# Dummy transposes only in the first part of the order, and later expected landings for the loads of tiles 9 and on

## The chip, the cores and the metric

The kernel runs on one core of a Trainium2 chip. The metric is the device time of one execution in microseconds (us), the median of several runs. TensorE is called PE here, its weight loads PEld, VectorE DVE, ScalarE ACT, GpSimd POOL and SyncE SP. A "q" behind a name (SPq) is the sequencer of that engine, which issues DMAs and serves semaphores.

## The reference

A linear attention with a decaying state runs over 768 steps of 4 batches and 8 heads; its output, 3072 tokens of 384 values, goes through a feed-forward layer with silu, and then through a routed layer, in which every token visits one of 8 experts:

```python
for t in range(S):
    cur = np.einsum('bhd,bhe->bhde', u[None] * kt, vt)
    y[:, :, t] = np.einsum('bhd,bhde->bhe', rt, state + cur)
    state = w[None, :, :, None] * state + np.einsum('bhd,bhe->bhde', kt, vt)
...
h = x @ w_in
x = (h * (1.0 / (1.0 + np.exp(-h)))) @ w_out
...
logits = x @ w_gate + modality_bias[modality_id]
e_idx = np.argmax(logits, axis=1)
gate_w = probs[np.arange(N), e_idx]
for e in range(E):
    h = np.maximum(x[mask] @ w1[e], 0.0)
    out[mask] = gate_w[mask, None] * (h @ w2[e])
```

x has 3072 rows; d_model is 384, the first hidden width 2048, that of an expert 1024.

## The kernel before, in words

**Tiles.** The tokens are cut into 24 tiles of 128, and three tiles form a group j (0 to 7). For each tile, the attention part turns a load A (L284: v and the transposed r and k, 768 KB, into one of the buffers AB_132, AB_133 and "stall") and a load B (L287: r and k in natural order, 192 KB for tiles below NZ = 9, 384 KB from there) into rows of x. The steps that matter here: L460 (DVE) and L464 (POOL) scale the two halves of A; L435 and L436 (POOL) multiply r, k and u, from load B; L439 (DVE) sums them; L480 and L548 (POOL) are two more elementwise steps; L487 (PE) forms the scores and L493 (DVE) writes them under the causal mask; L503 and L544 (PE) form the output and the state.

**The first layer.** For a group and each of 16 slices of the hidden width, L618 (PE) forms the hidden values in bank ph, in nine products, as each operand is split into a high and a low part; L622 and L623 (ACT) apply silu, L625 (DVE) makes the low part gl, and L637 (PE) adds nine products into the three accumulators pa_79 to pa_81. Groups 0 and 1 are computed in two halves of the slices; after the second half L653 (DVE) adds the accumulators to the first half's result in x2all.

**Routing.** L686 (PE) transposes x2all, L697 and L702 (PE) form the logits, L714 to L720 (DVE) choose the expert, L734 (POOL) counts, L739 and L740 (PE) turn counts into ranks. L764 (SP) stores the rows of x to the buffer x_rows in DRAM, three per group; L780 (POOL) scatters the token numbers to the lists of their experts.

**The expert stage.** Nine slots of 384 tokens, each of one expert: rows of x are gathered (POOL), L949 and L957 (PE) form the two products, L961 (ACT) or L963 (DVE) scales the result by the gate, and L966 (POOL) scatters 128 rows to the output by an indirect DMA. After them L1078 opens a loop over slots that did not fit into the nine; with these inputs it is not entered, but every engine meets at it.

**What sets the order.** The class Plan is a small scheduler which runs when the program is built. Every piece of work is added with an engine, a planned duration, a priority (lower goes first), its dependencies and the buffers that it takes and frees. `order` steps a clock, and each idle engine takes the ready piece of lowest priority. A piece with nbytes is a DMA: its planned landing follows a common stream of 260 KB per us plus a constant, and its consumers become ready only then. The planned start times are then the order in which the instructions are written (L1074), and each engine executes its own instructions in that order; nothing reorders them on the chip. A piece whose planned landing is earlier than the real one therefore stands in its engine's queue and blocks what is behind it.

**Dummy transposes.** L371 to L373 add 100 blocks of four 128 x 128 transposes of the identity with priorities from 900 on, so that the planned PE takes one wherever it has nothing else that is ready:

```python
for i in range(100):
    add("PE", 0.45, 900 + i, lambda i=i: [pe.transpose(bank(("w", i))[:, 0:128], ident, ident) for _ in range(4)],
        acq=[("ha"[i % 2], ("w", i))], rel=[("w", i)], lat=0.0)
```

Their results are never read. In the plan of the kernel before, 45 blocks start between 1.0 and 118.2 us and 55 between 742 and 771 us, all of them at the end of the expert stage.

Of the kernel before, what the change touches and what calls it, by code (L numbers as in the profile page):

```python
# [16 lines left out]
SP = mybir.EngineType.SP  # L17
# [25 lines left out]
NZ = 9  # L43
# [13 lines left out]
class Plan:  # L57
# [7 lines left out]
    def add(self, eng, dur, prio, fn, deps=(), acq=(), rel=(), lat=0.2, nbytes=0):  # L65
        o = Op()
        o.eng, o.dur, o.prio, o.fn, o.lat, o.nbytes = eng, dur, prio, fn, lat, nbytes
        o.deps = [d for d in deps if d is not None]
        o.acq, o.rel = list(acq), list(rel)
        o.n, o.after, o.left = len(self.ops), [], 0  # L70
        self.ops.append(o)
        return o

    def order(self):
# [6 lines left out]
        events, dma, t, done = [], 0.0, 0.0, []  # L81
# [4 lines left out]
        while True:  # L86
            moved = True
            while moved:
                moved = False
                for e in ENGINES:  # L90
                    if busy[e] > t + 1e-9 or not ready[e]:
                        continue
                    held, pick = [], None
                    while ready[e]:
                        x = heapq.heappop(ready[e])
                        need = {}
                        for p, _ in x[2].acq:
                            need[p] = need.get(p, 0) + 1
                        if all(len(self.free[p]) >= k for p, k in need.items()):
                            pick = x[2]  # L100
                            break
                        held.append(x)
                    for x in held:
                        heapq.heappush(ready[e], x)
                    if pick is None:
                        continue
                    o = pick
                    for p, key in o.acq:
                        self.slot[key] = (p, self.free[p].pop(0))
                    o.start = t  # L110
                    busy[e] = t + o.dur
                    end = t + o.dur + o.lat
                    if o.nbytes:
                        dma = max(dma, t + o.dur) + o.nbytes / 260e3
                        end = dma + 4.0
                    heapq.heappush(events, (busy[e], count, None))
                    heapq.heappush(events, (end, count + 1, o))
                    count += 2
                    done.append(o)
                    moved = True  # L120
# [19 lines left out]
def moe_rwkv_kernel(tc, ins, out):  # L140
# [142 lines left out]
    def load_A(n, s):  # L283
        sp.dma_start(AB[s][:, 0:AW], ins["av"][n])  # L284

    def load_B(n, s, w_=0):
        sp.dma_start(AB[s][:, AW + w_ * DM:], ins["rk"][n * C:(n + 1) * C, w_ * DM:])  # L287
# [52 lines left out]
    for i in range(NP):  # L340
        n = 1 << i
# [17 lines left out]
    def sl_(key):  # L359
        return P.slot[key][1]  # L360
# [47 lines left out]
    def attention(n):  # L408
# [5 lines left out]
        if n < 3:  # L414
            P.slot[kA] = ("tA", n)
            if n < 2:
                P.free["tA"].remove(n)
            oA, oB = gate((0.1, 0.2, 2.2)[n]), add("SP", 0.5, -49 + n, lambda: load_B(n, n, 1), nbytes=200e3)
        else:
            oA = add("SP", 0.6, z - 9, lambda: load_A(n, sl_(kA)), acq=[("tA", kA)], nbytes=786e3)  # L420
            oB = add("SP", 0.6, z - 8.9, lambda: load_B(n, sl_(kA), int(n < NZ)), [oA], nbytes=393e3 if n >= NZ else 197e3)
        relA = [kA] if n != 2 else []

        def f_V():
# [648 lines left out]
        expert(s)  # L1073
    with tc.manual_schedule():  # L1074
        for o in P.order():
            o.fn()
    tn = nc.values_load(tailn, min_val=0, max_val=NMAX - NSTAT + NA + 1)
    with tc.For_i(0, tn, 1) as i:  # L1078
        e_ids("t", lists[1], bass.ds(i + (NSTAT - 1 - NA), 1))
# [91 lines left out]
```

## Time and profile before

| | us |
|---|---|
| median of 3 runs | 808.32 (807.42 to 811.14) |
| the profiled execution | 806.15 |
| its span in the profile | 804.4 |
| PE busy with products | 791.2 (98%) |
| DVE, ACT, POOL busy | 425.7, 337.3, 227.9 |
| dummy transposes L372, on the chain that ended last | 5% of the span (3% into pa, 2% into ph) |

The profile is one execution. Its page gives the busy time of each engine, the span in 40 slices of 20.1 us with the clock that was granted to TensorE, and the groups of instructions. Behind it stand views of the trace: the waits of an engine by what ended them, the timeline of a stretch, and the sums of a stretch. The clock is written as a share of full speed. Rows of the views follow below, in the order in which the prediction comes to them.

### The profile page before, as it was taken

What the parts mean: (1) busy time and instruction counts of PE and PEld (TensorE: products, weight loads), DVE (VectorE), ACT (ScalarE), POOL (GpSimd) and SP (SyncE); (2) the same over time, 40 slices, a digit from 0 to 9 for tenths busy, and PEclk for the clock granted to TensorE, in tenths of its full rate; (3) what the DMA queues carried; (4) which work ended last, traced back from release to release, by engine and by line L of the source; (5) the groups of instructions that cost most, each with busy time, mean ns of one, the idle gap of its engine ahead of it and who ended that gap; (6) DMA issues with size and microseconds to landing.
All of it is one profiled execution on the core that took longest, in us unless ns stands there. A gap on an engine that the chain in (4) does not pass through costs nothing.

```text
span 804.4 us, 15749 instructions
## 1 busy us (share of the span) xinstructions
PE 791.2 (98%) x6348; PEld 760.0 (94%) x6348; DVE 425.7 (53%) x793; ACT 337.3 (42%) x726; POOL 227.9 (28%) x280
## 2 busy tenths in 40 slices
PE   8999999998999999999999999999999999999998
PEld 7998999987999999999999999999999999999998
DVE  7989965635534543644643522353866544654310
ACT  3566765443334334334334422364435434444200
POOL 5435302343423422522421203210432313220120
PEclk9999999998999999999999999999999999999999
DMA  6454433081511411411421024531675345500000
GB/s 245 153 177 184 167 119 108 28 79 44 90 59 59 91 60 60 89 60 61 85 65 59 11 22 180 224 120 68 217 217 187 128 135 199 196 28 1 30 35 2
DMA packets 23920, 83.27 MB, mean 104 GB/s; under 512 B 7659, under 2 KB 12152, under 8 KB 21538
## 3 DMA queue, kind: packets, MB, share of 16 engines
q1 hardware_dynamic: 19730, 72.55, 30.1%
q0 software_dynamic: 3968, 9.66, 3.6%
q8 instruction: 51, 0.84, 0.5%
q14 instruction: 27, 0.22, 0.2%
q10 hardware_dynamic: 144, 0.00, 0.0%
HBM read 78.92 MB, written 9.77 MB: 110 GB/s over the span
## 4 chain that ended last, share of the span: by engine, by line
PE 90%; DVE 4%; DMA 3%; issue 1%; ACT 1%; POOL 1%; DVEq 0%; POOLq 0%; SPq 0%; ACTq 0%
PE ph L618 24%; PE pa L637 23%; PE ph L949 13%; PE pa L957 12%; PE pt L503 4%; PE pa L372 3%; PE pt L487 3%; PE ph L372 2%; DMA xgb<-x_rows,it 2%; DMA AB<-in_av_dram 1%; PE pt L933 1%; PE ph L305 1%; PE pt L686 1%; PE pt L544 1%; PE pt L697 1%
## 5 line engine op out<-in xcount | busy, mean ns | idle before, releaser
L625 DVE TENSOR_TENSOR gl<-sg,gh 128x384 fp32r<-128x384 f32 x128 | 86.7, 677 | 136.4 <-ACT gh L623 135.9
L622 ACT ACTIVATE sg<-ph 128x384 f32<-128x384 f32 x128 | 63.0, 492 | 214.0 <-PE ph L618 205.6
L637 PE MATMUL pa<-Wh,gh 128*128 128x384 f32 x384 | 132.7, 346 | 0.0
L637 PE MATMUL pa<-Wh,gl 128*128 128x384 f32 x384 | 129.7, 338 | 0.5 <-DVE gl L625 0.4
L637 PE MATMUL pa<-Wl,gh 128*128 128x384 f32 x384 | 128.8, 335 | 0.0
L618 PE MATMUL ph<-xh,Wh 128*128 128x384 f32 x384 | 92.8, 349 | 0.0
L618 PE MATMUL ph<-xh,Wl 128*128 128x384 f32 x384 | 88.9, 339 | 0.1
L618 PE MATMUL ph<-xl,Wh 128*128 128x384 f32 x384 | 88.5, 338 | 0.0
L1034 ACT ACTIVATE gh<-ph 128x384 fp32r<-128x384 f32 (+1 forms) x66 | 32.7, 495 | 113.5 <-PE ph L949 112.9
L1036 DVE SCALAR_TENSOR_TENSOR gl<-ph,gh 128x384 fp32r<-128x384 f32 (+1 forms) x66 | 36.8, 558 | 81.1 <-ACT gh L1034 81.1
L637 PEld LDWEIGHTS pa<-Wh,gh 128*128 128x128 f32 x384 | 72.3, 188 | 3.2 <-issue 2.0
L637 PEld LDWEIGHTS pa<-Wh,gl 128*128 128x128 f32 x384 | 72.1, 188 | 1.2 <-DVE gl L625 1.2
L637 PEld LDWEIGHTS pa<-Wl,gh 128*128 128x128 f32 x384 | 72.3, 188 | 0.0
L618 PEld LDWEIGHTS ph<-xh,Wh 128*128 128x128 f32 x384 | 66.3, 189 | 4.8 <-issue 3.2
L966 POOL DMA_INDIRECT out_dram<-x2all,it x25 | 33.8, 1353 | 127.8 <-DVE x2all L963 114.6
L618 PEld LDWEIGHTS ph<-xh,Wl 128*128 128x128 f32 x384 | 69.3, 188 | 0.7 <-DVE Wl L596 0.7
L618 PEld LDWEIGHTS ph<-xl,Wh 128*128 128x128 f32 x384 | 69.5, 189 | 0.0
L929 DVE TENSOR_TENSOR Wl<-raw,Wh 128x1024 fp32r<-128x1024 f32 (+2 forms) x54 | 64.0, 1220 | 9.9 <-ACT Wh L925 9.9
L957 PE MATMUL pa<-Wh,gh 128*128 128x384 f32 x200 | 67.6, 338 | 0.8 <-DVE x2all L963 0.8
L957 PE MATMUL pa<-Wh,gl 128*128 128x384 f32 x200 | 67.5, 337 | 0.0
L957 PE MATMUL pa<-Wl,gh 128*128 128x384 f32 x200 | 67.0, 335 | 0.0
L475 ACT ACTIVATE atall<-ident,cs 128x128 f32<-128x128 f32 x176 | 57.2, 393 | 13.8 <-DVE cs L457 9.8
(226 smaller groups left out, 1385.2 us busy)
## 6 DMA issues: line engine op xcount, KB each, us to landing
raw<-in_we_dram SPq DMA_DIRECT2D x18, 1536.0 KB
AB<-in_av_dram SPq DMA_DIRECT2D x18, 768.0 KB
stall<-in_wio_dram SPq DMA_DIRECT2D x16, 768.0 KB
x_rows<-x2all SPq DMA_DIRECT2D x24, 192.5 KB
AB<-y_slow SPq DMA_DIRECT2D x16, 256.0 KB
stall<-in_av_dram SPq DMA_DIRECT2D x5, 768.0 KB
AB<-in_rk_dram SPq DMA_DIRECT2D x10, 384.0 KB
stall<-in_rk_dram SPq DMA_DIRECT2D x5, 384.0 KB
```

The source lines that it names most:

```text
L372: add("PE", 0.45, 900 + i, lambda i=i: [pe.transpose(bank(("w", i))[:, 0:128], ident, ident) for _ in range(4)], acq=[("ha"[i % 2], ("w", ...
L475: act.activation(atb[sl_(kT)][h % 2][:, h // 2, :], ident, AF.Copy, scale=cs[:, h:h + 1])
L618: pe.matmul(p, win(a, fc, kt), (xh, xl)[b_][j % 2][:, kt, :], start=i == 0, stop=i == len(ops) - 1)
L622: o_s = add("ACT", 0.5, s - 4, lambda: act.activation(sgb[sl_(kS)], hps[sl_(kH)][:, 0:n], AF.Silu), [o_g1], acq=[("sg", kS)])
L625: o_l = add("DVE", 0.55, s - 4, lambda: vv.tensor_tensor(glb[sl_(kG)][:, 0:n], sgb[sl_(kS)], ghb[sl_(kG)][:, 0:n].bitcast(F32), op=ALU.sub ...
L637: pe.matmul(a, g[:, ts], wout(wp_, fc), start=begin and i == 0, stop=end and i == 2)
L929: eng.tensor_tensor(e_view(buf, 1)[wi][sl], m2[s]["raw", wi][sl], e_view(buf, 0)[wi][sl].bitcast(F32), op=ALU.subtract)
L949: pe.matmul(p[:, i * n:(i + 1) * n], a[:, kt, fc * 128:(fc + 1) * 128], b_[xb][:, kt, 0:n], start=m == 0, stop=m == len(ops) - 1)
L957: pe.matmul(a[:, 0:DM], g[:, sl], wt_[:, fc, :], start=fc == 0 and m == 0, stop=fc == NFE - 1 and m == 2)
L966: i = gp.indirect_dma_start(out=out, out_offset=bass.IndirectOffsetOnAxis(ap=m2[s]["it"][:, t:t + 1], axis=0), in_=o, in_offset=None, boun ...
L1034: o2 = add("ACT", 0.62 if small else 0.5, z + k - 6, lambda kH=kH, kG=kG, m=m: act.activation(ghb[sl_(kG)][:, 0:m], hps[sl_(kH)][:, 0:m], ...
L1036: o3 = add("DVE", 0.7 if small else 0.57, z + k - 6, lambda kH=kH, kG=kG, m=m: vv.scalar_tensor_tensor(glb[sl_(kG)][:, 0:m], hps[sl_(kH)][ ...
```

## The change

Three things. First, a block of dummy transposes (priority 900 and above) is written only if its planned start is before 150 us: the first 45 stay and the last 55 are left out. The plan itself still holds them, so no other piece moves for that reason. Second, the constant behind a DMA's planned landing becomes 3.8 us plus the piece's own `lat`; that has the default 0.2, so most DMAs keep 4.0 us. Third, the A load of tiles 3 to 8 passes 0.2 and of tiles 9 to 23 passes 8.0, the B load 0.2 and 6.0: for tiles 9 and on, the planner expects the A load 7.8 us later and the B load 5.8 us later. What is loaded, and from where, is the same.

```diff
@@ -112,7 +112,7 @@
                     if o.nbytes:
                         dma = max(dma, t + o.dur) + o.nbytes / 260e3
-                        end = dma + 4.0
+                        end = dma + 3.8 + o.lat
@@ -417,8 +417,8 @@
-            oA = add("SP", 0.6, z - 9, lambda: load_A(n, sl_(kA)), acq=[("tA", kA)], nbytes=786e3)
-            oB = add("SP", 0.6, z - 8.9, lambda: load_B(n, sl_(kA), int(n < NZ)), [oA], nbytes=393e3 if n >= NZ else 197e3)
+            oA = add("SP", 0.6, z - 9, lambda: load_A(n, sl_(kA)), acq=[("tA", kA)], nbytes=786e3, lat=8.0 if n >= NZ else 0.2)
+            oB = add("SP", 0.6, z - 8.9, lambda: load_B(n, sl_(kA), int(n < NZ)), [oA], nbytes=393e3 if n >= NZ else 197e3, lat=6.0 if n >= NZ else 0.2)
@@ -1073,7 +1073,8 @@
         for o in P.order():
-            o.fn()
+            if o.prio < 900 or o.start < 150.0:
+                o.fn()
```

The order of PE's products is the same as before; besides the transposes that are gone, only the numbers of the banks pt change places here and there. On the other engines the work on tiles 9 and on moves. Three places follow; a name is out<-in with the buffer's number, then the shape.

DVE around the drains L653 of group 1, before (AB_132 holds tile 10 and AB_133 tile 11):

```order
L625 TENSOR_TENSOR gl_125<-sg_120,gh_122 128x384
L439 TENSOR_REDUCE cs_487<-AB_132 128x8
L440 TENSOR_SCALAR cs_487<-cs_487,flag 128x8
L625 TENSOR_TENSOR gl_126<-sg_119,gh_123 128x384
L460 TENSOR_TENSOR AB_133<-AB_133,Pt 128x512
L653 TENSOR_TENSOR x2all<-pa_80,x2all 128x384
L653 TENSOR_TENSOR x2all<-pa_79,x2all 128x384
L653 TENSOR_TENSOR x2all<-pa_81,x2all 128x384
L625 TENSOR_TENSOR gl_124<-sg_120,gh_121 128x384
```

The same place of DVE in the changed kernel:

```order
L625 TENSOR_TENSOR gl_125<-sg_120,gh_122 128x384
L460 TENSOR_TENSOR AB_132<-AB_132,Pt 128x512
L625 TENSOR_TENSOR gl_126<-sg_119,gh_123 128x384
L625 TENSOR_TENSOR gl_124<-sg_120,gh_121 128x384
L653 TENSOR_TENSOR x2all<-pa_80,x2all 128x384
L653 TENSOR_TENSOR x2all<-pa_79,x2all 128x384
L653 TENSOR_TENSOR x2all<-pa_81,x2all 128x384
L625 TENSOR_TENSOR gl_125<-sg_119,gh_122 128x384
L625 TENSOR_TENSOR gl_126<-sg_120,gh_123 128x384
L493 COPY_PREDICATED atall<-mask,pt_84 128x512
L493 COPY_PREDICATED atall<-mask,pt_83 128x512
L460 TENSOR_TENSOR AB_133<-AB_133,Pt 128x512
```

L460 on tile 11 has moved from ahead of the three drains to behind them, two L625 and the two L493 of tile 9. One L625 (gl_124) has moved from behind the drains to ahead of them, and L460 on tile 10 now stands where L439 on tile 10 stood.

SP's queue at the loads of tiles 10 (AB_132) and 11 (AB_133), as a difference; L425 is a load under a condition that follows the loads of a tile:

```order
 L284 DMA AB_132<-in_av_dram 128x1536
+L764 DMA x_rows<-x2all 128x385 x3
+L284 DMA AB_133<-in_av_dram 128x1536
 L287 DMA AB_132<-in_rk_dram 128x768
 L425 ISA
 L425 DMA AB_132<-y_slow 128x512
-L764 DMA x_rows<-x2all 128x385 x3
-L284 DMA AB_133<-in_av_dram 128x1536
 L287 DMA AB_133<-in_rk_dram 128x768
```

The B load of tile 10 used to follow its A load at once; now the row stores of group 0 and the A load of tile 11 stand between them. In the four next groups the row stores move in the same way from behind a tile's two loads to between its A and its B load.

PE at the last slot's second product L957, as a difference:

```order
 L957 MATMUL pa_81<-Wl_76,gh_123 128x384
 L957 MATMUL pa_81<-Wh_74,gl_126 128x384
-L372 MATMUL ph_77<-ident 128x128 x4
-L372 MATMUL ph_78<-ident 128x128 x4
-L372 MATMUL ph_77<-ident 128x128 x4
 L957 MATMUL pa_80<-Wh_73,gh_121 128x384
 L957 MATMUL pa_80<-Wl_75,gh_121 128x384
```

Twelve transposes ahead of the first of the last two sets of products are gone; four more go between the two sets, and 204 behind the last product, up to the loop head.

## Rows read from the trace of the kernel before

**Rows 1.** The page: its first line, and the granted clock in 40 slices.
```profile
span 804.4 us, 15749 instructions
PEclk9999999998999999999999999999999999999999
```

**Rows 2.** Waits of PE from 140 us on: us in total, times, longest.
```profile
PE pt L686 <- DVE x2all L653: 4.4, 1, 4.4
```

**Rows 3.** Timeline, 170 to 185 us: start, duration, instruction, idle time and its releaser.
```profile
173.97 0.33 SPq L284 DMA_DIRECT2D AB<-in_av_dram  x1
...
177.82 0.48 ACT L623 ACTIVATE gh<-ph 128x384 fp32r<-128x384 f32 x1
...
178.27 0.34 PE L637 MATMUL pa<-Wh,gl 128*128 128x384 f32 x1
...
179.50 0.69 PE L618 MATMUL ph<-xl,Wh 128*128 128x384 f32 x3
...
183.29 0.69 DVE L460 TENSOR_TENSOR AB<-AB,Pt 128x512 f32<-128x512 f32 x1 [6.72 <-DMA AB<-in_av_dram]
...
184.02 1.49 DVE L653 TENSOR_TENSOR x2all<-pa,x2all 128x384 f32<-128x384 f32 x3
...
184.63 1.15 PEld L686 LDWEIGHTS pt<-ident,x2all 128*128 128x128 f32 x6 [4.76 <-DVE x2all L653]
```

**Rows 4.** Sums of three stretches: busy us of each engine, PEclk, DMA share, GB/s.
```profile
core 0: us, PE busy (x) PEld busy (x) DVE busy (x) ACT busy (x) POOL busy (x), PEclk, DMA share, GB/s
180.00:184.00 4.00, 0.19 (x2) 0.00 (x0) 0.69 (x1) 0.49 (x1) 0.66 (x1) 0.84 0.55 218
184.00:188.00 4.00, 3.37 (x13) 3.37 (x14) 3.75 (x5) 1.25 (x3) 3.92 (x4) 0.50 0.01 2
188.00:192.00 4.00, 4.00 (x30) 3.65 (x30) 0.36 (x1) 1.48 (x3) 0.63 (x1) 0.81 0.00 0
```

**Rows 5.** Timeline of the end, 772 to 801 us.
```profile
772.47 0.58 ACT L961 ACTIVATE x2all<-pa,gt 128x384 f32<-128x384 f32 x1 [0.49 <-PE pa L957]
...
772.62 1.41 PEld L372 LDWEIGHTS ph<-ident 128*128 128x128 f32 x12
...
774.00 0.19 PEld L957 LDWEIGHTS pa<-Wh,gh 128*128 128x128 f32 x1
...
776.02 0.53 PEld L372 LDWEIGHTS pa<-ident 128*128 128x128 f32 x4
...
778.55 8.40 PEld L372 LDWEIGHTS pa<-ident 128*128 128x128 f32 x76
...
779.82 0.98 POOL L966 DMA_INDIRECT out_dram<-x2all,it  x1 [2.69 <-DVEq L1078]
...
800.56 0.60 PE L372 MATMUL pa<-ident 128*128 128x128 f32 x4
```

**Rows 6.** Line L966 of the whole run: its DMAs from issue to landing.
```profile
DMA to landing us min/median/max: 2.6/3.4/9.0
```

**Rows 7.** Line L1078: ns min/median/max of its semaphore steps, first and last start.
```profile
L1078 POOLq EVENT_SEMAPHORE  x15: 17/43/16713, 780.1 to 799.7; - x15
L1078 PEldq EVENT_SEMAPHORE  x13: 51/51/51, 801.2 to 803.0; - x13
```

**Rows 8.** Timeline of PE, 73.5 to 75.5 us.
```profile
74.74 0.44 PE L637 MATMUL pa<-Wh,gl 128*128 128x384 f32 x1 [0.43 <-DVE gl L625]
```

**Rows 9.** Sums of a stretch that holds only dummy transposes; columns as in rows 4.
```profile
790.00:800.00 10.00, 10.00 (x94) 10.00 (x93) 0.00 (x0) 0.00 (x0) 0.00 (x0) 1.00 0.01 2
```

**Rows 10.** Timeline, 183 to 203 us: POOL, DVE and PEld.
```profile
183.34 1.77 POOL L464 TENSOR_TENSOR AB<-AB,Qt 128x512 f32<-128x512 f32 x1 [11.94 <-DMA AB<-in_av_dram]
...
187.32 1.31 POOL L480 TENSOR_TENSOR AB<-AB,PKt 128x384 f32<-128x384 f32 x1
...
192.37 1.36 DVE L493 COPY_PREDICATED atall<-mask,pt 128x512 f32<-128x512 uint32 x2 [0.18 <-PE pt L487]
...
196.35 0.75 POOL L734 TENSOR_TENSOR oha<-oha,r_ohb 128x8 bf16<-128x8 bf16 x3 [7.72 <-DVE r_ohb L719]
...
202.08 0.10 PEld L739 LDWEIGHTS <-tri 128*128 128x128 bf16 x1 [0.16 <-issue]
```

## The prediction, made before the changed kernel ran

> **What bounds the kernel now.** I read the page's first lines, then who made TensorE wait, then the two stretches where it did not do useful work. TensorE (PE) is busy nearly all of the 804.4 us [rows 1], so only two things can move the time: work taken off PE, and waits of PE. In the page's row of granted clock (40 slices of 20.1 us), one slice in the middle is below full, the tenth, 181 to 201 us. The list of PE's waits after 140 us has one entry of more than a microsecond: L686, the transposes that begin routing for group 1, waits 4.4 us for L653 on VectorE (DVE), the drain of the second-half sums [rows 2].
>
> [rows 3] show how. SyncE issues the load of tile 11 into AB_133 at 173.97. The next instruction in DVE's queue is L460 on that tile; it idles 6.72 us and starts at 183.29, when the load lands, 9.3 us after its issue. The three drains L653 stand behind it in the same queue and start at 184.02, though the last product they read started at 178.27. PE ran out at 179.50 + 0.69 = 180.19 and loads weights again at 184.63. After that its clock stands at 0.50, the lower of its two levels (1.2 of 2.4 GHz), for 184 to 188, and 0.81 on average for 188 to 192 [rows 4].
>
> The other stretch is the end. The last useful product starts loading before 778.55; from there to 800.56 + 0.60 = 801.16 PE does nothing but dummy transposes of L372 [rows 5], 204 of them. The last store of rows (L966) is issued by GpSimd (POOL) at 779.82, its DMAs land 2.6 to 9.0 us after issue, 3.4 in the median [rows 6], and at the loop head L1078 POOL waits once for 16.7 us, to 799.7, so since 783.0 [rows 7]. That is 3.2 us after the last issue, in agreement with the landing. PE's own steps at L1078 begin at 801.2, and the span ends at 804.4: 3.2 us after PE's last transpose.
>
> **The change part by part.** First, the transposes after planned time 150. The plan holds 100 blocks of four; 45 stand before that time and stay in the same places of PE's order, 55 (220 transposes) go. They were on the path that sets the end.
>
> After the last product: the end passes from PE at 801.16 to the landing of the last store at 783.0, with the same 3.2 us behind the last arrival. That is 801.16 - 783.0 = 18.2 us. Bounds: if the landing takes 9.0 instead of 3.2 us, the gain is 12.4; if 2.6, it is 18.8. If the end hangs on the release at 799.7 instead of on PE at 801.2, 4.7 us follow it instead of 3.2 and the gain is 16.7. I take 18.2, since PE's steps are the ones that begin at 801.2.
>
> Between the last products: twelve transposes from 772.62, then the first set of 12 products with weights at 774.00. Those products write pa_80, which ScalarE (ACT) drains from 772.47 to 773.05 [rows 5]; a hand-over took 0.1 us at the drain of [rows 3] (184.02 plus a third of 1.49, against 184.63). So PE can start at 773.15, a gain of 0.85; the four at 776.02 took 0.53 and nothing hides them. Together 1.4 us; bounds 0.5 (the wait is as long as the transposes) and 1.4. In exchange PE idles about 0.5 us at 772.6. It idled 0.43 us at 74.3 [rows 8], and that slice shows full clock [rows 1], so I charge nothing for the clock.
>
> A rule of the Trainium skill bears on this place: "TensorE: Matmul & The Clock Gate", Part 4, says that the full clock does not engage for transposes, since they do not count as busy in the same way. The trace does not agree: 10 us of nothing but transposes, 790 to 800, ran with the clock at 1.00 [rows 9]. By the rule the dummies here are worthless and their loss costs no clock; by the row they hold it, and their loss could cost it, which is a rival below.
>
> Second, the expected landings. The planner now expects the A load (L284) of tiles 9 and on 7.8 us later and the B load (L287) 5.8 us later. No product moves on PE: its order differs only in the transposes that are gone and in bank numbers of pt. What moves is DVE's, POOL's, ACT's and SyncE's work on the tiles. At the place of the stall, L460 on AB_133 now stands behind the three drains, two L625 and two L493. Ahead of the drains stands one more L625; its input comes from ACT's L623, 177.82 + 0.48 = 178.30 [rows 3], so it ends at about 179.0 (0.7 for itself, as L460 takes on a larger tile). The first two drains, at 0.5 each (1.49 / 3), end at 180.0, before PE needs them at 180.2. The wait is gone: 4.4 us. With it goes the clock: 3.37 us busy at half speed in 184 to 188 is 1.7, and 4 x 0.19 in 188 to 192 is 0.76 [rows 4], together 2.4 us. Bounds of the two: 0 (the wait moves elsewhere) and 6.8.
>
> What is late next? L460 on AB_133 now comes after the two L493 of tile 9, which ended at 193.7 [rows 10] and move up with PE by 6.8 to about 186.9; the landing at 183.29 is 3.6 us earlier. DVE no longer waits. On SyncE the three row stores L764 and the A load of tile 11 now precede the B load of tile 10, which before was issued at once after its A load. It must wait for AB_133 to come free, so it goes out just after 173.97 and lands with or after tile 11's A load, at 183.3 to about 185 (384 KB at the 218 GB/s of 180 to 184 [rows 4] are 1.8 us). POOL's L435 on tile 10 waits for it, and behind it in POOL's queue stand L464, L436, L480, L548 and then L734, the routing count for which PE waits at L739. The four elementwise steps took from 183.34 to 187.32 + 1.31 = 188.6, 5.3 us, in the trace [rows 10]; L548, one more such step, I put at the 1.3 of L480. From 185 on they end at about 191.6, and L734 (0.75) at 192.3. L739 stood at 202.08, moved up by 6.8 to 195.3 [rows 10]. So 3.0 us of cover are left, and I charge nothing; with the cover gone, up to 6.8 us come back. In the four later rounds the row stores only slip between the A and B load of one tile; their sums are ready by then, and the B load is 1.3 us later ahead of work that PE needs some 20 us later. Nothing.
>
> The Trainium skill, "DMA: Bandwidth & Descriptors", section "Queues, rings and completion order", says that one issuer's descriptors are consumed in ring order on each DMA engine. By it, the B load cannot pass the A load now in front of it, and the landing is the later end, 185; no run here shows the new order, and the sum is the same by either end.
>
> **Sum.** 18.2 + 1.4 + 4.4 + 2.4 = 26.4 us, all against the profiled execution, which took 806.15 us (1.75 outside the span): 779.7. The median of the runs shown, 808.32, is 2.2 above it, so the forecast for a median is 781.9.
>
> **The rivals.**
> 1. *The stall is handed on.* The landing that took 9.3 us is not understood, and the B load of tile 10 now sits behind it. If it lands more than 3.0 us after 185, PE waits at L739 instead of L686, and its clock falls as before: up to 6.8 us return, 788.7. For it: POOL serves its queue in order, so one late tile holds the routing count. Against: the cover just worked out.
> 2. *The end is set by the last landing at its worst*, 9.0 us [rows 6], or by the longer tail: 781.9 + 1.5 to + 5.8, so 783.4 to 787.7. For it: that landing is now alone on the path. Against: this very store landed in 3.2.
> 3. *The clock falls at the end.* Without dummies the last 24 products (774.00 to 776.02, and 2.0 more) run at 1.2 GHz and cost 4.1 us more: 786.0. For it: 4.4 us of idleness lowered the clock. Against: 0.43 did not.
> 4. *Slower.* SyncE is the place: in five rounds the B load now stands behind L764, which waits for routing sums of DVE. If those come after the A load is issued by more than the B load can spare, POOL waits for the B load in each round, and PE after it. At 6.8 us a round that is 34 us against the 26.4 won, but the first stall's 6.8 are counted in both: 808.3 - 26.4 + 34 = 816. It decides from four such rounds on. Against it: L764 stands in SyncE's order where its sums are done before the A load of the next tile is due, and PE's only wait of over a microsecond is the one of group 1 [rows 2], so the later rounds have more to spare than that one had.
> 5. *Nothing gained*: the transposes fall where the end waits anyway. POOL's wait of 16.7 us [rows 7] speaks against it.
>
> **How the numbers follow.** Forecast 0.70; rivals 1 to 5: 0.12, 0.10, 0.04, 0.02, 0.02. The range reaches up to rival 1 in full, 788.7, which takes in 2 and 3; down, the runs shown spread 0.9 below their median, the landing bound gives 0.6, and if the 2.2 between profile and median shrinks by as much as the spread above it (2.8), little is left of it: 777.5. A difference under 0.5% can't be told from none here. All but rivals 4 and 5 are far below 804.3: faster 0.96, same 0.02, slower 0.02.
>
> **What would show it.** In the changed kernel's trace: no wait of L686 for L653, clock 1.00 in the slices around 181 to 201; L460 on tile 11 after L493 with no idle time before it; no wait of PE at L739; PE's last instruction near 770, the last L966 about 1 us later, the span's end some 6.4 us after that. A stall at L739 or L503 in 180 to 240, a half clock in the last ten microseconds, or more than 5 us between the last store's issue and its landing would make it wrong by the prices above.

## The result, and the profile after

The changed kernel takes 784.01 us (median of four runs, 780.99 to 784.60), the kernel before 809.73 (median of four, 807.42 to 813.01): a ratio of 0.9672, with an interval of 0.9627 to 0.9717, or 25.7 us less. The forecast was 781.9 in a range of 777.5 to 788.7. The profiled execution of the changed kernel took 784.13 us, that of the kernel before 806.15; these two differ by 22.0 us, in their spans too.

The page's first line and its row of granted clock (40 slices, here of 19.6 us), which answer to [rows 1]:

```profile
span 782.4 us, 15315 instructions
PEclk9999999999999999999999999999999999999998
```

The waits of PE over the whole run (us in total, times, longest), which answer to [rows 2]:

```profile
PE pa L330 <- DVE neq L329: 3.2, 1, 3.2
PE ph L618 <- issue: 1.2, 1, 1.2
PE pa L957 <- issue: 0.8, 1, 0.8
PE pa L637 <- DVE gl L625: 0.4, 1, 0.4
PE pt L503 <- issue: 0.4, 1, 0.4
```

L686 is gone from it, and so is L739. The first entry lies in the first microseconds, as in the kernel before. New are entries whose releaser is "issue": PE stood still and waited for nothing that the profile shows.

The place of the old stall, 177 to 200 us: start, duration, instruction, in brackets the idle time before it and its releaser. This answers to [rows 3] and [rows 10]:

```profile
178.10 0.19 PEld L618 LDWEIGHTS ph<-xh,Wh 128*128 128x128 f32 x1
...
179.63 0.69 PE L618 MATMUL ph<-xh,Wh 128*128 128x384 f32 x3 [1.20 <-issue]
...
179.85 0.33 SPq L284 DMA_DIRECT2D AB<-in_av_dram  x1
...
182.90 1.49 DVE L653 TENSOR_TENSOR x2all<-pa,x2all 128x384 f32<-128x384 f32 x3
...
184.19 0.76 PEld L686 LDWEIGHTS pt<-ident,x2all 128*128 128x128 f32 x6
...
187.42 1.02 POOL L435 TENSOR_TENSOR AB<-AB 128x384 f32<-128x384 f32 x1 [13.63 <-DMA AB<-in_rk_dram]
...
191.28 1.21 DVE L460 TENSOR_TENSOR AB<-AB,Pt 128x512 f32<-128x512 f32 x1
...
194.25 0.76 POOL L734 TENSOR_TENSOR oha<-oha,r_ohb 128x8 bf16<-128x8 bf16 x3
...
199.51 0.10 PEld L739 LDWEIGHTS <-tri 128*128 128x128 bf16 x1 [0.16 <-issue]
```

L686 follows the drains without a wait. L460 on tile 11 runs at 191.28, behind them, with no idle time in its brackets. The B load of tile 10 ends POOL's wait at 187.42, 2.4 us later than the 185 that the prediction took; L734 ends at 195.0 and L739 comes at 199.5, so the cover held. What is new is the row at 179.63: PE loads weights at 178.10 and multiplies 1.5 us later.

The granted clock of the changed kernel at the place of the old stall and near the start (the columns are those of [rows 4]):

```profile
12.00:16.00 4.00, 4.00 (x43) 3.67 (x41) 2.49 (x4) 2.11 (x8) 1.27 (x1) 1.00 0.61 228
16.00:20.00 4.00, 3.95 (x29) 3.36 (x30) 4.00 (x7) 1.24 (x3) 3.09 (x2) 0.51 0.71 210
20.00:24.00 4.00, 4.00 (x44) 3.61 (x46) 2.94 (x5) 0.00 (x0) 0.05 (x1) 0.63 0.12 26
...
184.00:188.00 4.00, 4.00 (x28) 3.93 (x28) 0.95 (x2) 2.52 (x6) 0.58 (x1) 1.00 0.87 330
188.00:192.00 4.00, 4.00 (x47) 3.43 (x47) 2.93 (x4) 0.77 (x2) 3.93 (x4) 1.00 0.00 0
```

The half clock at 184 to 192 of [rows 4] is 1.00 now. But this execution stood at 0.51 and 0.63 from 16 to 24 us. The page's row of slices can't show that (it has a 9 there in both kernels); the same stretches of the kernel before do:

```profile
16.00:20.00 4.00, 4.00 (x48) 3.42 (x46) 4.00 (x6) 0.93 (x2) 3.14 (x2) 1.00 0.65 206
20.00:24.00 4.00, 4.00 (x81) 3.56 (x81) 4.00 (x8) 2.50 (x4) 0.99 (x1) 1.00 0.23 36
```

The end, which answers to [rows 5]:

```profile
770.50 0.19 PEld L957 LDWEIGHTS pa<-Wh,gh 128*128 128x128 f32 x1 [0.47 <-ACTq L1079]
...
774.60 0.34 PE L957 MATMUL pa<-Wh,gl 128*128 128x384 f32 x1
...
774.97 0.62 DVE L963 TENSOR_SCALAR x2all<-pa,gt 128x384 f32<-128x384 f32 x1 [3.82 <-issue]
...
775.87 0.98 POOL L966 DMA_INDIRECT out_dram<-x2all,it  x1 [1.33 <-DVEq L1079]
```

The last product is followed by its scaling, the last store at 775.87, and the span's end at 782.4, 6.5 us after that issue.

To see where the 22.0 us are, I cut each span at starts of ACT's silus (L622, the 1st, 32nd, 36th, 75th, 81st, 91st and 128th) and the last expert activation (L1034), each a row in the timeline. The segments, in us:

| segment | before | after | gained |
|---|---|---|---|
| start to silu 1 | 33.85 | 36.91 | -3.06 |
| 1 to 32 | 136.25 | 136.22 | 0.03 |
| 32 to 36 (the old stall) | 18.99 | 13.69 | 5.30 |
| 36 to 75 | 161.26 | 160.28 | 0.98 |
| 75 to 81 | 22.09 | 22.67 | -0.58 |
| 81 to 91 | 41.22 | 41.99 | -0.77 |
| 91 to 128 | 134.96 | 134.27 | 0.69 |
| 128 to the last L1034 | 222.76 | 222.75 | 0.01 |
| last L1034 to the end | 33.02 | 13.62 | 19.40 |

The end gave what was forecast for it, 19.4 of 19.6. The stall gave 5.3 of 6.8. Two segments for which the prediction had nothing gained 0.98 and 0.69. Against them stand 3.06 at the start, at the half clock, and 1.35 at two places in the middle.

### The profile page after: what moved, and what is told of

The parts are those of the page before. It is cut to its first block, busy times and chain, and to the rows that moved or that the text cites. A ratio compares the mean times of both kernels' runs of the same rounds, so it can differ in the third digit from the quotient of the medians.

```text
span 782.4 us, 15315 instructions
## 1 busy us (share of the span) xinstructions
PE 768.5 (98%) x6128; PEld 736.9 (94%) x6128; DVE 403.8 (52%) x793; ACT 337.5 (43%) x726; POOL 222.4 (28%) x280
## 5 line engine op out<-in xcount | busy, mean ns | idle before, releaser
L622 ACT ACTIVATE sg<-ph 128x384 f32<-128x384 f32 x128 | 63.0, 492 | 216.4 <-PE ph L618 193.2
L625 DVE TENSOR_TENSOR gl<-sg,gh 128x384 fp32r<-128x384 f32 x128 | 79.2, 619 | 145.5 <-ACT gh L623 136.8
L618 PE MATMUL ph<-xh,Wh 128*128 128x384 f32 x384 | 92.3, 348 | 1.2 <-issue 1.2
L618 PE MATMUL ph<-xh,Wl 128*128 128x384 f32 x384 | 88.5, 338 | 0.0
L618 PE MATMUL ph<-xl,Wh 128*128 128x384 f32 x384 | 88.1, 337 | 0.0
L1034 ACT ACTIVATE gh<-ph 128x384 fp32r<-128x384 f32 (+1 forms) x66 | 32.6, 495 | 113.5 <-PE ph L949 104.6
L618 PEld LDWEIGHTS ph<-xh,Wh 128*128 128x128 f32 x384 | 65.9, 188 | 6.1 <-issue 4.5
L618 PEld LDWEIGHTS ph<-xh,Wl 128*128 128x128 f32 x384 | 68.9, 187 | 0.5 <-DVE Wl L596 0.5
L966 POOL DMA_INDIRECT out_dram<-x2all,it x25 | 33.8, 1354 | 124.8 <-DVE x2all L963 111.1
L618 PEld LDWEIGHTS ph<-xl,Wh 128*128 128x128 f32 x384 | 69.1, 187 | 0.0
L957 PE MATMUL pa<-Wh,gh 128*128 128x384 f32 x200 | 67.5, 338 | 1.0 <-issue 0.8
L957 PE MATMUL pa<-Wh,gl 128*128 128x384 f32 x200 | 67.4, 337 | 0.0
L957 PE MATMUL pa<-Wl,gh 128*128 128x384 f32 x200 | 67.0, 335 | 0.0
```

The source lines that it names most:

```text
L618: pe.matmul(p, win(a, fc, kt), (xh, xl)[b_][j % 2][:, kt, :], start=i == 0, stop=i == len(ops) - 1)
L622: o_s = add("ACT", 0.5, s - 4, lambda: act.activation(sgb[sl_(kS)], hps[sl_(kH)][:, 0:n], AF.Silu), [o_g1], acq=[("sg", kS)])
L625: o_l = add("DVE", 0.55, s - 4, lambda: vv.tensor_tensor(glb[sl_(kG)][:, 0:n], sgb[sl_(kS)], ghb[sl_(kG)][:, 0:n].bitcast(F32), op=ALU.sub ...
L957: pe.matmul(a[:, 0:DM], g[:, sl], wt_[:, fc, :], start=fc == 0 and m == 0, stop=fc == NFE - 1 and m == 2)
L966: i = gp.indirect_dma_start(out=out, out_offset=bass.IndirectOffsetOnAxis(ap=m2[s]["it"][:, t:t + 1], axis=0), in_=o, in_offset=None, boun ...
L1034: o2 = add("ACT", 0.62 if small else 0.5, z + k - 6, lambda kH=kH, kG=kG, m=m: act.activation(ghb[sl_(kG)][:, 0:m], hps[sl_(kH)][:, 0:m], ...
```

## The experiments

Ratios are to the kernel before, run on the same chip; its medians were 807.11 us beside the first four kernels, 811.00 beside the next four, 807.18 beside the next three and 810.17 beside the last. A ratio is not the quotient of the two medians; it differs from it by up to 0.003.

**The tail alone.** The kernel before with the filter on the dummy transposes and nothing else:

```diff
-            o.fn()
+            if o.prio < 900 or o.start < 150.0:
+                o.fn()
```

> The kernel before with only the filter on the dummy transposes; the expected landings stay as they were. Theory (the parts add up): the tail gives 18.2 and the sixteen transposes between the last products 1.4, so 19.6 us less than the kernel before, a ratio of 0.976; the stall of L686 behind L460 on tile 11 is still there, about 4.4 us, with the clock at 0.50 behind it. Rival (the dummies held the clock for the last products): the last 24 products run at half clock and the gain is 15.5 us. Rival (the end hangs on something else than PE): less than 5 us.

Measured: 788.70 us (784.52 to 794.66), a ratio of 0.9802 (0.9752 to 0.9852). The profiled execution, the fastest, took 784.52; from the last L1034 to the end it took 13.74 us against 33.02, a gain of 19.3. So the term of the tail, 19.6, holds, and neither rival does: the clock is 1.00 to the last product, and the end did move. The stall is there, in this kernel's waits of PE:

```profile
PE pt L686 <- DVE x2all L653: 3.4, 1, 3.4
```

The sums of the two stretches around it show the clock, third from the right:

```profile
180.00:184.00 4.00, 1.07 (x8) 0.92 (x9) 2.38 (x5) 0.56 (x3) 2.37 (x2) 1.00 0.47 186
184.00:188.00 4.00, 4.00 (x31) 3.72 (x31) 2.26 (x3) 2.13 (x5) 2.87 (x3) 1.00 0.01 2
```

PE stood still for 3.4 us and the clock stayed at 1.00, where 4.4 us of standing still were followed by 0.50 [rows 4]. So the 2.4 us for the clock are not part of every execution that stalls. The median gain, 18.4 us (807.11 - 788.70; by the ratio 16.0, within 12 to 20), is less than the tail alone gives in the profile, and the other three runs have lower mean clocks (0.988 to 0.994 against 0.997): some of its executions lose time in places that its one trace doesn't show. Even that trace, with the orders of the kernel before, has two stops of PE "on issue", of 0.8 us at an L503 and 1.1 us at an L544.

**The landings alone.** The changed kernel with all 100 blocks:

```diff
-            if o.prio < 900 or o.start < 150.0:
-                o.fn()
+            o.fn()
```

> The changed kernel with all 100 blocks of dummy transposes; only the expected landings are new. Theory: the stall of 4.4 us at L686 and the half clock behind it are gone, 6.8 us less than the kernel before, a ratio of 0.9916; PE's last dummy ends about 795, 22 us behind the last product. Rival (the stall moves on to L739 or elsewhere): a ratio within 0.003 of 1. In both, a dip of the clock at 16 to 23 us, as the changed kernel's profile shows and that of the kernel before does not, is expected to come and go between executions of one program (3.2 us when it is there); if it belongs to the change, it stands here too and not in e1_tail.

Measured over ten runs: 804.38 us (800.60 to 807.00), a ratio of 0.9969 (0.9950 to 0.9989). That is 2.5 us, and neither the theory's 6.8 nor nothing. The profiled execution is the fastest of the ten, with a mean clock of 1.000, and lies 5.6 us below the profiled one of the kernel before in its span (798.8 against 804.4): the stall's segment is 12.86 us, 6.1 less than before, and the segment from silu 81 to 91 is 42.59, 1.4 more. The dip at 16 to 23 us isn't in its trace. Over the ten runs the time rises as the mean clock falls: 1.000 goes with 800.60 and 801.84, 0.996 with 806.81 and 807.00. The one execution of the kernel before that had 1.000 beside them took 803.70, so at equal clock the landings give some 2 to 3 us. So they do take away the stall, but most of the forecast 6.8 is missing from the median; where the executions with lower clocks lose it isn't shown, since the one trace is of the fastest.

**Only the A load's landing.**

```diff
-... nbytes=393e3 if n >= NZ else 197e3, lat=6.0 if n >= NZ else 0.2)
+... nbytes=393e3 if n >= NZ else 197e3, lat=0.2)
```

> The changed kernel with the later landing for the A load alone; the B load of tiles 9 and on is expected as before. The order of SyncE is that of the changed kernel and L460 on tile 11 stands behind the three drains, as there. Theory (the stall hung on the place of L460 alone): same time as the changed kernel within 0.3%, a ratio of 0.967 to the kernel before, and no wait at L686. Rival (the B load's landing is needed too, POOL's work on tile 10 holds L734): a wait of PE at L739 of 2 us or more, and 3 to 7 us over the changed kernel.

Measured: 785.42 us (782.43 to 790.12), a ratio of 0.9756 (0.9704 to 0.9809). The orders of PE and SyncE are those of the changed kernel; on the other three engines the work on tiles 9 and on has moved part of the way back. No wait at L686 and none at L739, so the place of L460 does it and the B load's landing isn't needed for it. The ratio is worse than the changed kernel's, with overlapping intervals; the two longest of the four runs have mean clocks of 0.988 and 0.992, the other two 0.997. PE stood still for 2.0 us at an L618 "on issue", in the same few instructions as in the changed kernel (the row at 179.63 above).

**The changed kernel again.** The same program, to see its spread.

> The changed kernel unaltered, to see how its executions spread. Theory (the half clock at 16 to 23 us in its first profile was chance, since the instructions up to there stand in the same order as before the change): executions with a mean granted clock of about 0.997 (only the idle end is counted) at 779 to 781 us and others at 0.990 to 0.995 some 3 us longer; a median of 780 to 785, a ratio of 0.965 to 0.973. Rival (the change brings the dip): every execution shows 0.992 or less.

Measured: 788.31 us (782.18 to 788.77), a ratio of 0.9702 (0.9649 to 0.9756). The profiled execution (span 786.5) has full clock at 16 to 24 us: silu 1 starts at 33.84, as in the kernel before (33.85). So the 3.06 us at the start are not the change's: the same program has them in one execution and not in another, and every engine's instructions up to there stand in the order of before. The rival is out as well, with mean clocks of 0.991 to 0.998. The median, however, is above the expected 780 to 785, and the trace shows where one of these executions (788.26 us) lost its time. In its timeline, PE stops inside L503:

```profile
406.14 1.04 PE L503 MATMUL pt<-atall,AB 128*32 128x128 f32 x26
409.64 0.70 PE L503 MATMUL pt<-atall,AB 128*32 128x128 f32 x6 [2.46 <-issue]
```

26 of 32 products are done, then nothing for 2.46 us, though the six that follow need nothing that the 26 did not. The clock then falls, by the sums of the stretches:

```profile
408.00:412.00 4.00, 2.36 (x14) 2.02 (x15) 0.56 (x1) 0.49 (x1) 1.92 (x3) 0.92 0.00 0
412.00:416.00 4.00, 4.00 (x29) 3.47 (x29) 0.71 (x2) 0.12 (x1) 0.88 (x1) 0.65 0.35 81
```

The segment from silu 81 to 91 takes 45.77 us instead of 41.22. A second stop, 2.3 us at the first L618 sets behind tile 8's L544 (176.36 to 178.67), also has a fall of the clock behind it (0.66 from 180 to 184), and the old stall's segment is 2.9 us longer than in the first profile (16.63 against 13.69). What the first profile had lost at the start, this one lost in the middle.

What was late? In the stretch before the stop, the DMA queues show a single packet, of the queue that the profile names "instruction", 0.02 MB; its time is given as a share of 16 engines over the 5 us from 402 to 407:

```profile
q8 instruction: 1, 0.02, 4.5%
```

4.5% of 16 times 5 us are 3.6 us. It starts at 402.4, and PE resumes at 409.64. Read in the same way, the packet ahead of that L503 took 3.4 to 3.6 us in six profiles that stop there (the changed kernel in both, the landings alone, A alone, all tiles but 11, and the one with 12 blocks, the last two below), and 1.5 us in three that don't (the kernel before, the tail alone, and tile 11 alone, below). It fits that PE ran out of instructions because their load came late. It isn't shown: no view names what PE waited for, and why the packet is slow stays open. Three things speak against the packet's time as the whole cause. The six stops last 0.4 to 3.6 us behind packets that took nearly the same time. Packets as slow pass without a stop: this one in the kernel before (459 to 464 us), where PE has no stop "on issue" anywhere,

```profile
q8 instruction: 1, 0.02, 4.2%
```

took 3.4 us, and one in the last kernel below 4.1 us. And the stop of 1.2 us that the kernel with tile 11 alone has at 211 us stands behind a packet of 1.5 us. What the six do share is the new order of SyncE's loads and stores, together with PE's stream as the 45 blocks or the 12 leave it; the kernel with the A load alone stops there although its DVE, ACT and POOL work in another order.

**All tiles but 11.** The old landings for tile 11 alone, the new ones for the rest:

```diff
-... lat=8.0 if n >= NZ else 0.2)
+... lat=8.0 if n >= NZ and n != 11 else 0.2)
-... lat=6.0 if n >= NZ else 0.2)
+... lat=6.0 if n >= NZ and n != 11 else 0.2)
```

> The changed kernel, but with the old expected landings for tile 11 alone. SyncE's order is that of the changed kernel; L460 on tile 11 stands ahead of the three drains L653 again, as in the kernel before. Theory (the place of this one instruction was the stall): PE waits 3 to 5 us at L686 for L653 again and the time is 3 to 7 us over the changed kernel run beside it. Rival (the later B load and the other moves took the stall away): no wait over 1 us at L686 and the same time within 0.3%.

Measured: 786.26 us (784.54 to 787.71), a ratio of 0.9703 (0.9663 to 0.9742), beside 0.9702 for the changed kernel again. The stall is back in the waits of PE, as the theory has it,

```profile
PE pt L686 <- DVE x2all L653: 3.8, 1, 3.8
```

and with it the fall of the clock, in the sums of this kernel's stretches:

```profile
180.00:184.00 4.00, 0.32 (x2) 0.33 (x3) 1.63 (x3) 0.43 (x1) 1.61 (x1) 0.92 0.67 267
184.00:188.00 4.00, 4.00 (x20) 3.97 (x19) 2.97 (x4) 1.65 (x5) 3.89 (x5) 0.65 0.00 0
```

The segment takes 18.84 us. So the place of tile 11's work is the stall, and by the waits it is L460 on DVE. Yet the time is the same as that of the changed kernel on this chip, and below that of the tail alone (0.9802, on another chip): in the profiles, the 2.2 us more at this segment (18.84 against 16.63) are met by 3.6 us less from silu 81 to 91 (42.16 against 45.77). The theory's 3 to 7 us did not appear in the total.

**Tile 11 alone.** The new landings for tile 11, the old ones for all others:

```diff
-... lat=8.0 if n >= NZ else 0.2)
+... lat=8.0 if n == 11 else 0.2)
-... lat=6.0 if n >= NZ else 0.2)
+... lat=6.0 if n == 11 else 0.2)
```

> The changed kernel with the later landings for tile 11 alone; all other tiles are expected as in the kernel before. L460 on tile 11 stands behind the three drains. Theory (this one tile is the whole gain of the landings): no wait of PE over 1 us at L686 and a time within 3 us of the changed kernel, a ratio of 0.964 to 0.972. Rival (the other tiles' moves give something too): 0.973 or more. If the stop at L503 near 405 us comes with the later tiles' new places, it is gone here, and the stretch takes 41.2 us.

Measured: 780.47 us (779.61 to 780.91), a ratio of 0.9657 (0.9618 to 0.9696). Its waits of PE from the second entry on:

```profile
PE pa L637 <- issue: 1.2, 1, 1.2
PE pt L544 <- issue: 1.0, 1, 1.0
PE pa L957 <- issue: 0.8, 1, 0.8
```

And the instruction packet ahead of the same L503, in its DMA queues from 401 to 406 us:

```profile
q8 instruction: 1, 0.02, 1.9%
```

No wait at L686, no stop at L503 (the segment takes 41.22 us), and the packet took 1.9% of 16 times 5 us, 1.5 us. The four runs lie within 1.3 us, with clocks of 0.997 and 0.998; the changed kernel's lie within 3.6 and 6.6 us. SyncE's order is that of the kernel before. But PE's is not: one set of nine L618 moves from between the transposes L686 to behind them, so this is not the plain opposite of the run with all tiles but 11. What the two show together is less than the theory: tile 11's landing alone is enough for the ratio of the changed kernel, but so are all the others, with the stall in place (0.9703). In this pair the stall follows tile 11 and the stop near 405 us follows the other tiles' new places; how the time divides between them the totals don't show.

**PE's stream shifted.** 18 warm-up transposes at the start instead of 50:

```diff
-    for _ in range(50):
+    for _ in range(18):
         pe.transpose(hps[1][:, 0:128], ident, ident)
```

> The changed kernel with 18 instead of 50 warm-up transposes at the very start (L305), all 45 blocks kept: every later instruction of PE stands 64 places earlier in its stream. Theory (PE's stops without a releaser, at the second half of L503 near 405 us and at the first L618 behind tile 8's L544 near 178 us, come at fixed places of PE's instruction stream, where the next load of instructions arrives late): the stop at L503 is gone or elsewhere, and the stretch in which the kernels with the new landings and all 45 blocks took 42.0 to 45.8 us takes 41.2. Rival (the stop belongs to the new order of VectorE and ScalarE): 42.0 us or more there again, at the same L503.

Measured: 782.56 us (781.98 to 784.20), a ratio of 0.9681 (0.9642 to 0.9720). The segment from silu 81 to 91 takes 41.16 us and the stop at L503 is gone, with the engines' orders unchanged: the rival, that the stop belongs to the orders alone, falls for this place. At the other place it is not settled. PE waits 1.6 us there for a silu of ACT, which itself waited 6.8 us for PE, and the old stall's segment (14.62) is no shorter than in the changed kernel's first profile. This execution, too, has half clock near the start (0.50 from 12 to 24 us), and silu 1 starts at 36.67.

**Which dummies are worth their time.** Four kernels that keep fewer of the 45 early blocks: none; only those planned from 30 us on (20); only those before 30 us (25); only those from 30 to 56 us (12).

```diff
-            if o.prio < 900 or o.start < 150.0:
+            if o.prio < 900:
...
+            if o.prio < 900 or 30.0 < o.start < 150.0:
...
+            if o.prio < 900 or o.start < 30.0:
...
+            if o.prio < 900 or 30.0 < o.start < 56.0:
```

> The changed kernel without any of the 100 blocks of dummy transposes. Theory (the first 45 hold the clock in the first 120 us): the granted clock falls to 0.50 there for tens of us and the time is 10 to 30 us over the changed kernel. Rival (they hold nothing that counts, since PE waits for loads and for VectorE there anyway): within 4 us of the changed kernel, either way; in that case the dip of the clock at 16 to 23 us costs nothing either.

> The changed kernel without the first 25 blocks of dummy transposes as well (planned start before 30 us); the 20 blocks planned from 31 to 118 us stay. The kernel without any block stood at the same point at 33.5 us, with half the clock, where the changed kernel stood at 36.9 with half the clock and others at 33.1 to 33.8 with the full one. Theory (in the first 30 us the transposes only cost where the clock falls, and hold nothing that PE would need): 0 to 4 us less than the changed kernel, 777 to 783, and less spread. Rival (without them the clock stays low beyond 36 us): 2 us or more over the changed kernel.

> The changed kernel with only the first 25 blocks of dummy transposes (planned start before 30 us); the 20 blocks planned from 31 to 118 us go as well. Theory: dips of the clock at 52 to 56 and 68 to 80 us, as in the kernel without any block, and 1 to 3 us over the changed kernel. Rival (PE waits for VectorE there anyway): the same time within 0.3%.

> The changed kernel with only the 12 blocks of dummy transposes planned between 30 and 56 us; the first 25 and the last 8 of the 45 go as well. Theory (the last 8 only stand in PE's way: the kernels without them took 0.6, 0.4 and 0.45 us less in three stretches between 85 and 125 us): 1 to 1.5 us less than the kernel that keeps the 20 blocks from 30 us on, 777 to 780, a ratio of 0.958 to 0.963. Rival (they hold the clock for the products at 70 to 80 us): a dip there and a ratio of 0.965 or more.

| blocks kept | us | ratio (interval) | silu 1 starts at |
|---|---|---|---|
| 45, changed kernel | 784.01 | 0.9672 (0.9627 to 0.9717) | 36.91 |
| 45, changed kernel again | 788.31 | 0.9702 (0.9649 to 0.9756) | 33.84 |
| none | 780.41 | 0.9676 (0.9636 to 0.9715) | 33.49 |
| 20, from 30 us on | 780.31 | 0.9633 (0.9596 to 0.9670) | 32.00 |
| 25, before 30 us | 779.23 | 0.9609 (0.9573 to 0.9645) | 36.91 |
| 12, from 30 to 56 us | 783.96 | 0.9702 (0.9661 to 0.9744) | 32.55 |

The theory for "none", 10 to 30 us more, is wrong, and the rival holds. The clock does fall without them:

```profile
16.00:20.00 4.00, 3.72 (x44) 2.94 (x44) 4.00 (x6) 0.91 (x1) 2.66 (x2) 0.50 0.70 203
20.00:24.00 4.00, 4.00 (x50) 3.46 (x46) 2.72 (x6) 1.99 (x3) 0.73 (x1) 0.50 0.48 129
```

Yet silu 1 starts at 33.49: at half clock, PE has time enough for the real work of the first 30 us, but not for the transposes as well. That is how the half clock cost the first profile of the changed kernel 3 us. With the early transposes the clock holds in some executions, and where it falls all the same they are what makes it dear. For 20 blocks the theory holds (780.31, four runs within 2.8 us). For 25 blocks the theory (1 to 3 us more) is wrong: this kernel has the lowest median of all, though its profile has the half clock near the start. For 12 blocks the rival's ratio is right, 0.970, and so is its dip (0.63 from 76 to 80 us), but stops of 2.0 and 3.6 us at the two known places are in the time as well. Beside the changed kernel on the same chip (0.9702), the kernels with 20 and with 25 blocks are some 8 and 9 us faster. Neither stops at the L503 near 405 us (41.16 in that segment for both), and leaving out blocks shifts PE's stream as well, so these runs don't part the two reasons.

**The two together.** Tile 11 alone, with the 25 blocks before 30 us:

```diff
-            if o.prio < 900 or o.start < 150.0:
+            if o.prio < 900 or o.start < 30.0:
-... lat=8.0 if n >= NZ else 0.2)
+... lat=8.0 if n == 11 else 0.2)
-... lat=6.0 if n >= NZ else 0.2)
+... lat=6.0 if n == 11 else 0.2)
```

> The later landings for tile 11 alone, and of the dummy transposes only the first 25 blocks (planned start before 30 us). Theory (what both parts save is stops and transposes at different places, so it adds up): the stall at L686 stays away, no stop of over 1 us at L503 near 400 us, and 776 to 780 us, a ratio of 0.957 to 0.963. Rival (where the stops fall changes with every instruction that goes, so that the sum of the parts says nothing): stops of 1 to 4 us at new places and a ratio of 0.965 or more.

Measured: 780.80 us (779.30 to 782.25), a ratio of 0.9636 (0.9603 to 0.9669). No stop "on issue" of a microsecond and no stall, but not below its parts (0.9657 and 0.9609): the gains don't add up, and the intervals overlap too much to say more. Its profile has the half clock near the start (silu 1 at 36.89).

## Why the prediction was right, and where it was not

- **The tail, 18.2 us, and the last products, 1.4.** Right in size: the last store was issued 0.9 us after L963 began, and the span ended 6.5 us after the issue (6.4 were forecast). The 783.0 in it was misread: 799.7 [rows 7] is the start of POOL's last step, and its long wait runs from 782.7 to 799.4 in the trace, together with ACT's and DVE's. For the landing of each of the last four stores the traces of the kernel before and of the tail alone have 2.6 us; the changed kernel's gives none. The sum hardly depends on it, as it uses 6.4 us from the issue to the end. From the last L1034 to the end the gain is 19.4 us. The clock was still 1.00 while the last products ran (768 to 776 us), so the rival of half clock at the end is out. That transposes alone hold the clock, as [rows 9] had it, is not the whole of it: near the start, where blocks of them stand between short products, it fell in spite of them.
- **The stall, 4.4 us.** Right in mechanism: L686's wait went, came back when tile 11's landing alone was put back (3.8 us), and stayed away when tile 11's landing alone was moved. Its size differs from profile to profile (4.4, 3.4, 3.8). Why the load lands so late stays open: with SyncE's loads in the same order, the load behind it (L425) could start 9.3, 7.8, 8.4 and 13.9 us after its issue (the kernel before, the tail alone, and the two kernels with tile 11 alone).
- **The clock behind it, 2.4 us.** The term was taken as certain and is not: one stalled execution fell to 0.65 (all tiles but 11), another not at all (the tail alone). It is usual, though: of the 13 executions of the kernel before on that chip, 12 had mean clocks of 0.995 to 0.998, as its profile has (0.995). It should have been a term with a bound at zero of its own.
- **The later tiles, "nothing".** This is the step that failed, if in the small. The moves of tiles 9, 10 and 12 on bring PE no wait for another engine, as forecast. But every kernel with new landings for the later tiles, all 45 blocks and PE's stream unshifted took 0.8 to 4.6 us more from silu 81 to 91, by a stop of PE inside L503 that has no releaser in the profile. That is a part of why the landings alone are worth 2.5 us and not 6.8; their own trace has 1.4 us of it, and the rest isn't shown. No rival of the prediction had PE stop without anything to wait for.
- **The handed-on stall** (rival 1) did not come, though the loads were later than its cover allowed for: the A load of tile 11 was issued at 179.85, not just after 173.97. It had landed by 186.4, when L425 behind it starts, and the B load, behind it as forecast, ended POOL's wait at 187.4 and not at 185. L734 was still done 4.5 us before L739, as PE itself came to L739 4.2 us later than forecast (199.5 against 195.3).
- **Slower SyncE** (rival 4): PE has no wait for work on a B load in any later round.
- **The 2.1 us between forecast and median.** The sum was made against one profiled execution, and that one (806.15) was shorter than all four timed runs of the kernel before; the changed kernel's had 3.06 us of half clock at the start that its second profile has not. Medians differ by 25.7 us, near the sum of 26.4; the profiles by 22.0. With the pair of profiles alone one would have looked for a single cause of 4.4 us that isn't there. That 25.7 lies so near 26.4 is in part luck: the two parts alone gave 18.4 and 2.5 us, 20.9 together, and the changed kernel run again gave 22.7 (811.00 - 788.31).

## What to carry to other kernels

Where engines run in a fixed order, a planner's expected landing decides who stands behind whom; try it first for the one load that is late: here tile 11 alone was enough for the time of the changed kernel, with the least spread. Filler work at the end of the program is time like any other. Filler at the start did not bring the first silu forward: with 45 blocks and full clock it came at 32.6 to 33.9 us, with none and half clock at 33.5, and with 45 blocks and half clock at 36.7 and 36.9. Before the difference of two profiles is explained, run one of the kernels twice and cut both spans into the same segments.

## What the runs showed of the hardware that was not expected

- PE stops of 0.4 to 3.6 us without a releaser, in the same few instructions in several kernels, and gone from one place when PE's stream was shifted by 64 instructions. Where the instruction packet ahead of L503 near 405 us took 3.4 us or more, PE stopped there; at 1.5 us it did not. At other places slow packets passed without a stop, and a stop came behind a packet of 1.5 us.
- Around these stops, signals of work that PE had long finished come late: in the changed kernel, L622 on the L618 that ended at 176.9 started at 180.1, with SyncE's L284 and DVE's L559 at 179.9, just after PE resumed at 179.6. PE need not stop for it. In the kernel before, tile 8's L544 ended at 170.56, and the two that wait for it, DVE's L559 and the A load of tile 11 [rows 3], started at 174.01 and 173.97, while PE went on:

```profile
170.00 0.56 PE L544 MATMUL pt<-AB 128*48 128x48 f32 x16
174.01 0.72 DVE L559 TENSOR_TENSOR S<-pt,S 48x192 f32<-48x192 f32 x2 [4.55 <-PE ph L618]
```

  In the kernel with PE's stream shifted both started 0.1 us behind that L544 (ended 173.53), but an L622 came at 182.2 on an L618 that had ended at 176.9, which is the wait of 1.6 us told above:

```profile
173.65 0.72 DVE L559 TENSOR_TENSOR S<-pt,S 48x192 f32<-48x192 f32 x2 [1.22 <-PE pt L544]
182.22 0.49 ACT L622 ACTIVATE sg<-ph 128x384 f32<-128x384 f32 x1 [6.77 <-PE pa L637]
```

  Whether this lateness made tile 11's load land late in the kernel before isn't shown: with the load issued at 173.61 here, L425 behind it still started only at 186.24.
- The length of a stop does not tell whether the clock falls behind it: after 2.5, 3.8 and 4.4 us it fell (0.65, 0.65 and 0.50 over 4 us), after 3.4 it stayed at 1.00; after about 2.0 us at the first L618 sets behind tile 8's L544 it stayed in one kernel (the A load alone, 1.00 from 176 to 184) and fell in another (12 blocks, 0.74 and 0.83 over 4 us each). Near the start, executions of one program, with PE busy throughout, had 1.00 and 0.51.
- Transposes alone also raise the clock, by their spacing. From 3.2 to 11.5 us PE runs only the 50 transposes L305, but for one product of 4 columns. In the kernel before, 11 of them fall into 5 to 7 us and 20 into 9 to 11 us; one followed another after 213 ns at first and after 109 ns from 8.7 us on, as the two levels of the clock would have it (the clock column has 1.00 in both stretches):

```profile
5.00:7.00 2.00, 2.00 (x11) 2.00 (x10) 1.90 (x7) 0.00 (x0) 1.69 (x3) 1.00 1.02 421
9.00:11.00 2.00, 2.00 (x20) 2.00 (x19) 1.89 (x2) 0.10 (x1) 1.46 (x1) 1.00 0.72 300
```
